# A new order list for a fused attention and two feed-forward stages, and products of 384 and 512 tokens

## The chip, the cores and the metric

The kernel runs on one core of a Trainium2 chip. TensorE (PE) multiplies matrices, VectorE (DVE) and ScalarE (ACT) work on elements and can read PE's results from PSUM, GpSimd (POOL) works on elements in SBUF alone, and SyncE (SP) issues nearly all DMAs. Each engine works through its own list of instructions in order and waits on semaphores for the others. The metric is the time of one execution in microseconds (us); the kernel before took 354.3 us, the median of three runs (353.45 to 354.36).

## The reference, cut to what matters

Two sequences of 448 tokens, 12 heads of 64, model width 768, inner width 1024. Causal attention, then a feed-forward stage that mixes each token with the one before it, then a feed-forward stage with a convolution of width 3 along the tokens:

```
attn = softmax(causal(q @ k.T / 8)) @ v            # per head
x    = attn, heads side by side                    # (2, 448, 768)
xk   = mu_k * x + (1 - mu_k) * x_prev              # x_prev: the token before
xr   = mu_r * x + (1 - mu_r) * x_prev
x2   = sigmoid(xr @ w_r) * (relu(xk @ w_k)**2 @ w_v)
h    = relu(x2 @ w_in)
out  = (h * sigmoid(conv3(h))) @ w_out
```

All five weight matrices arrive as 64-bit floats and are turned into 32-bit ones on the chip.

## The kernel before, in words

Attention is cut into 12 jobs: two sequences times six pairs of heads. A job's steps carry the names that stand in the order list. `Lk` and `Lv` load q, k and v (SP). `kqT` transposes q and k on PE, `kC.k` and `kC.q` copy the result out of PSUM. `sc.2` and `sc.1` are the scores on PE in 64x64 tiles, in two parts. `red` (DVE) adds the mask and finds the row's extreme, `exp` (ACT) exponentiates and sums, `rec` (DVE) inverts the sums, `norm` scales the probabilities, mostly on POOL. `T.a` and `T.b` transpose the probabilities on PE, `C.aX` and the like copy them out, `V.a` and `V.b` multiply by v. From the result `mP` (a scaling) and `mD` (a scaled addition) make the mixed inputs: kind 1 for xr, kind 0 for xk.

For the feed-forward products every number is split into a high and a low part. `mH` and `mL` make those of xr, `k0:H` to `k11:L` those of xk (the numbers 0 to 5 are the six chunks of 128 features of the first sequence, 6 to 11 of the second). A chunk of a result then takes three products on PE: high by high, high by low, low by high. A weight slice `w0` to `w5` (of w_r) and `w6` to `w8` (the first three of w_k) has steps too: `L` loads it, `a` (ACT) to `e` build the 32-bit floats, `h` and `l` split them. `pr3.1.4` stands for w_r's slice 3, token part 1, chunk 4: three products. `sr3.1` copies the finished bank out of PSUM. `E0` to `E3` are the first two slices of w_k, 18 products each, for two token parts. `W` steps are products with nobody to read them, which keep PE running. A letter behind a slash names the engine: a for ACT, v for DVE, p for POOL.

What sets the order is the list ORDER: `issue` takes its tokens one by one, and PE, ACT, DVE and POOL keep that order under a manual schedule (lines 624 to 627). The loads in it are kept in order on SP as well. Buffers are handed out from short lists as steps ask for them: eight PSUM banks, three buffers for raw q and k, four for v, two for raw weights, two for converted ones, four for split ones. Behind ORDER the rest of w_k, w_v and the second stage follow: for w_k and w_v the scheduler places the instructions, for the last stage a second list, LATE.

The other w_k and all w_v products are cut into a part of 512 tokens and one of 384 (lines 672 to 680). The w_r products and E0 to E3 are cut by sequence, 448 and 448:

```
TOK = [slice(b * S, (b + 1) * S) for b in range(B)]
```

Of the kernel before, what the change touches and what calls it, by code (L numbers as in the profile page):

```python
# [19 lines left out]
def kernel(  # L20
# [457 lines left out]
    class Slice:  # L478
# [22 lines left out]
        0:Lk W0 sm:L W*2 0:kqT 0:kC.k/a sm:a 1:Lk 0:kC.q/v W*2 0:sc.2 W*1 1:kqT sm:n 0:red.0 0:red.5 0:red.2 0:red.3  # L501
        0:exp.0 0:sc.1 1:kC.k/v 2:Lk 0:exp.5 1:kC.q/a 0:exp.2 1:sc.2 0:red.6 0:exp.3 0:red.1 0:red.4 0:exp.1 0:exp.4
        2:kqT 1:red.5 1:red.2 2:kC.k/v 1:red.0 0:exp.6 1:red.3 3:Lk 1:sc.1 2:kC.q/a 0:Lv 0:rec sm:T 2:sc.2 1:exp.2
        1:exp.5 0:norm.2/p 1:red.1 1:red.4 3:kqT 1:exp.1 1:exp.0 0:norm.4/p 1:exp.3 sm:C 0:norm.1/p 1:red.6 3:kC.q/v
# [4 lines left out]
        0:V.b 1:T.b 4:kC.q/a 3:exp.6 2:norm.5/p 2:norm.1/p 4:sc.1 3:red.1 2:norm.3/p 3:exp.5 0:V.a 3:red.3 1:C.bY/v
        2:norm.6/p w1:a 2:norm.0/p 2:norm.2/p w1:b/p 3:red.2 3:red.4 1:C.bX/v 1:C.aX/v 4:red.4 3:exp.3 2:norm.4/p  # L510
        0:mP.1/a 5:Lk 3:exp.4 4:red.1 2:T.a 3:exp.2 4:sc.2 2:T.b 3:exp.1 0:mP.0/v 2:C.aX/a 4:red.6 2:C.aY/a 3:rec
        w1:c 3:norm.3/p 3:norm.0/p 5:kqT 4:exp.1 4:red.3 4:red.0 2:C.bX/v 4:exp.4 5:kC.k/v 0:mD.1 3:norm.5/p
# [551 lines left out]
```

## Time and profile before

| | us |
|---|---|
| median of three runs | 354.3 (353.45 to 354.36) |
| profiled execution, from its first to its last instruction (its time as a run isn't recorded) | 351.6 |
| PE busy | 345.2 (98%) |
| DVE busy | 306.9 (87%) |
| ACT busy | 235.1 (67%) |
| POOL busy | 90.3 (26%) |
| last value product of attention ends | 90.03 |
| first product of w_k starts | 120.5 |

The profile is of one execution. Its span runs from the first to the last instruction; the rest of a run's time lies around it. Matmuls overlap, so a stretch in which PE is busy throughout can still hold short waits; those are seen in the chain of work that ended last, which is followed back from the end: its pieces are counted from the start of one instruction to that of the next, so that a piece divided by its count gives the pace of a product.

### The profile page before, as it was taken

What the parts mean: (1) busy time and instruction counts of PE and PEld (TensorE: products, weight loads), DVE (VectorE), ACT (ScalarE), POOL (GpSimd) and SP (SyncE); (2) the same over time, 40 slices, a digit from 0 to 9 for tenths busy, and PEclk for the clock granted to TensorE, in tenths of its full rate; (3) what the DMA queues carried; (4) which work ended last, traced back from release to release, by engine and by line L of the source; (5) the groups of instructions that cost most, each with busy time, mean ns of one, the idle gap of its engine ahead of it and who ended that gap; (6) DMA issues with size and microseconds to landing.
All of it is one profiled execution on the core that took longest, in us unless ns stands there. A gap on an engine that the chain in (4) does not pass through costs nothing.

```text
span 351.6 us, 7196 instructions
## 1 busy us (share of the span) xinstructions
PE 345.2 (98%) x2682; PEld 309.2 (88%) x2682; DVE 306.9 (87%) x629; ACT 235.1 (67%) x515; POOL 90.3 (26%) x149
## 2 busy tenths in 40 slices
PE   7999999999999999999999999999999999999996
PEld 7678788888999998998889999988988999999995
DVE  2999999999889878989999998997998999897741
ACT  2999999999533276767786464354756877766501
POOL 3386986667435000000000000000000000368100
PEclk9999999999999999999999999999999999999999
DMA  5686597442033155347455434543232200379623
GB/s 132 146 222 144 127 222 213 90 116 93 7 95 106 66 180 181 121 148 240 142 187 171 156 101 173 179 143 128 89 103 79 89 2 0 67 134 202 138 91 135
DMA packets 63228, 45.33 MB, mean 129 GB/s; under 512 B 34752, under 2 KB 62156, under 8 KB 63192
## 3 DMA queue, kind: packets, MB, share of 16 engines
q1 hardware_dynamic: 59352, 40.68, 38.7%
q0 software_dynamic: 2912, 3.96, 6.6%
q8 instruction: 21, 0.34, 0.4%
q10 hardware_dynamic: 928, 0.23, 0.3%
q14 instruction: 15, 0.12, 0.1%
HBM read 38.17 MB, written 2.75 MB: 116 GB/s over the span
## 4 chain that ended last, share of the span: by engine, by line
PE 95%; DVE 1%; DMA 1%; POOL 1%; SPq 1%; issue 1%; ACT 0%; POOLq 0%
PE pk L66 17%; PE pv L66 17%; PE pr L66 13%; PE A L66 7%; PE po L391 6%; PE s L321 4%; PE B L66 4%; PE c L66 2%; PE Yb L363 2%; PE D L66 2%; PE Xa L363 2%; PE W L561 1%; PE q L300 1%; PE ph5l L66 1%; PE ph6l L66 1%; PE ph4l L66 1%
## 5 line engine op out<-in xcount | busy, mean ns | idle before, releaser
L887 POOL DMA_DIRECT2D s<-g x12 | 12.7, 1177 | 194.9 <-ACT st L87 188.6
L343 ACT ACTIVATE p<-e,st 128x448 f32<-128x448 f32 (+6 forms) x84 | 42.1, 507 | 1.7 <-DVE st L334 1.5
L72 POOL TENSOR_SCALAR p<-p,st 128x64 f32<-128x64 f32 (+6 forms) x70 | 34.6, 512 | 20.7 <-DVE st L334 11.4
L334 DVE CUSTOM_DVE_ANT_0 e<-s,mask 128x192 f32<-128x192 f32 (+6 forms) x84 | 31.6, 415 | 0.4 <-ACT p L343 0.2
L391 PE MATMUL po<-pt,v 128*64 128x128 f32 (+4 forms) x384 | 24.0, 277 | 0.0
L807 DVE SCALAR_TENSOR_TENSOR cv<-hT,cw,cv 128x448 f32<-128x448 f32 x32 | 21.5, 681 | 2.7 <-ACT cv L804 2.6
L391 PEld LDWEIGHTS po<-pt,v 128*64 128x64 f32 x384 | 20.0, 137 | 3.3 <-issue 0.3
L321 PE MATMUL s<-kT,qT 64*64 64x384 f32 (+6 forms) x336 | 22.1, 386 | 0.5 <-DVE kT L79 0.2
L321 PEld LDWEIGHTS s<-kT,qT 64*64 64x64 f32 x336 | 14.9, 132 | 6.6 <-ACT qT L79 0.7
L343 ACT ACTIVATION_READ_ACCUMULATOR p<-e,st 128x1 f32 x84 | 16.3, 194 | 0.0
L91 POOL TENSOR_TENSOR xr<-m,xr 128x448 fp32r<-128x448 f32 x10 | 12.0, 1198 | 2.1 <-ACT xr L87 1.7
L87 ACT ACTIVATE x<-xv 128x512 fp32r<-128x512 f32 (+1 forms) x12 | 6.8, 573 | 8.1 <-DVE xv L706 8.0
L811 ACT ACTIVATE cv<-cv 128x448 f32<-128x448 f32 x16 | 9.1, 571 | 3.2 <-DVE cv L807 3.2
L999 ACT ACTIVATE o<-A 128x384 f32<-128x384 f32 x3 | 1.5, 491 | 14.7 <-PE A L66 14.6
L804 ACT ACTIVATE cv<-hT,cw 128x448 f32<-128x448 f32 x16 | 10.7, 668 | 0.5 <-DVE g L91 0.3
L813 DVE TENSOR_TENSOR cv<-cv,hT 128x448 f32<-128x448 f32 x16 | 9.9, 621 | 1.2 <-ACT cv L811 1.2
L91 DVE TENSOR_TENSOR k<-a,k 128x512 fp32r<-128x512 f32 (+2 forms) x16 | 9.9, 619 | 0.0
L66 PE MATMUL pv<-k,wv0hl 128*128 128x512 f32 (+1 forms) x48 | 9.9, 364 | 0.0
L66 PE MATMUL pv<-k,wv4hl 128*128 128x512 f32 (+1 forms) x48 | 9.8, 363 | 0.0
L66 PE MATMUL pv<-k,wv2hl 128*128 128x512 f32 (+1 forms) x48 | 9.8, 363 | 0.0
L66 PE MATMUL pv<-k,wv3hl 128*128 128x512 f32 (+1 forms) x48 | 9.8, 363 | 0.0
L66 PE MATMUL pv<-k,wv5hl 128*128 128x512 f32 (+1 forms) x48 | 9.8, 363 | 0.0
(516 smaller groups left out, 1105.0 us busy)
## 6 DMA issues: line engine op xcount, KB each, us to landing
rqk<-in_q_dram SPq DMA_DIRECT2D x24, 112.0 KB, 2.8
rqk<-in_k_dram SPq DMA_DIRECT2D x22, 112.0 KB, 3.0
v<-in_v_dram SPq DMA_DIRECT2D x24, 96.0 KB, 3.0
s<-g POOLq DMA_DIRECT2D x12, 192.0 KB, 3.8
wo6raw<-g POOLq DMA_DIRECT2D x8, 192.0 KB, 4.8
wv0raw<-in_moe_w_v_dram SPq DMA_DIRECT2D x1, 1024.0 KB, 4.8
wv1raw<-in_moe_w_v_dram SPq DMA_DIRECT2D x1, 1024.0 KB, 4.9
wv2raw<-in_moe_w_v_dram SPq DMA_DIRECT2D x1, 1024.0 KB, 5.0
```

Source lines behind the costliest of these rows:

```text
L66: nc.tensor.matmul(ps_out, x, y, start=first and i == 0, stop=last and i == 2, skip_group_check=more,)
L72: nc.gpsimd.tensor_scalar(out_, in_, s, 1.0, ALU.mult, ALU.mult)
L91: e.tensor_tensor(out_, x, f32(h), ALU.subtract)
L321: nc.tensor.matmul(held[self.name(f"s{f}")][1][h, o:z], qT[r, i * LO:(i + 1) * LO], kT[r, :(i + 1) * LO], start=True, stop=True,)
L334: nc.vector.tensor_tensor_reduce(t[:, :w], used(self.name(f"s{f}"))[:, o:z], mask[:, S - w:], -SCALE, 3e38, ALU.add, ALU.min, self.st[:, 0 ...
L343: nc.scalar.activation(p[:, :w], self.s[i][:, :w], AF.Exp, bias=self.st[:, 0, i:i + 1], scale=-1.0, accum_out=self.st[:, 1, i:i + 1],)
L363: nc.tensor.transpose(o[:, u * LO:(u + 1) * LO], self.p[i][r, k0:k0 + P], ident[r, r])
L391: nc.tensor.matmul(self.T["po"][j * D:(j + 1) * D, 1 + i * LO - z:1 + (i + n) * LO], self.v[:, kc, j], self.T["pt"][:, a - z:a + n * LO], ...
L804: nc.scalar.activation(a, x[:, 0:S], AF.Copy, scale=cw[:, f:f + 1])
L807: nc.vector.scalar_tensor_tensor(a, x[:, j:S + j], cw[:, j * NF + f:j * NF + f + 1], a, ALU.mult, ALU.add)
L813: (nc.gpsimd if eng == "p" else nc.vector).tensor_tensor(a, a, hc, ALU.mult)
L887: nc.gpsimd.dma_start(out=dst, in_=f32(x), accum_op=ALU.add)
```

## The change

The list ORDER is replaced by another one with the same 712 steps. Only their order, the engine behind the slash and the places of the loads differ. Two lines of each:

```
-        0:Lk W0 sm:L W*2 0:kqT 0:kC.k/a sm:a 1:Lk 0:kC.q/v W*2 0:sc.2 W*1 1:kqT sm:n 0:red.0 0:red.5 0:red.2 0:red.3
-        sr3.0/v w8:d pr5.0.5 w8:e E1 w7:e w7:h w7:l/v E2 sr0.1/a w8:h sr5.0/v w8:l/v E3
+        W0 W*2 0:Lk sm:L 0:kqT 0:kC.k/v 1:Lk sm:a sm:n 2:Lk 3:Lk 0:kC.q/a W*1 W*2 0:sc.2 0:red.3 0:exp.3 0:red.2
+        pr5.0.5 w6:l/p E0 k8:H/p k8:L/p k6:L/p k7:L/p k10:H/a sr5.1/a k11:L/p k10:L/p E3 E1 sr5.0/a E2 w8:l/p
```

And the w_r products and E0 to E3 take token parts of 384 and 512, across the border of the sequences:

```
+    PART = [slice(0, 3 * P), slice(3 * P, NT)]
+
+    def width(t):
+        return t.stop - t.start
...
     def xr_products(e, b, c):
         if c == 0:
             bank(f"pr{e}_{b}", 1)
-        products(held[f"pr{e}_{b}"][1][:, :S], [slices[e].t], xr, TOK[b], NC, c)
+        t = PART[b]
+        products(held[f"pr{e}_{b}"][1][:, :width(t)], [slices[e].t], xr, t, NC, c)
...
-        copy(eng, sr[e][:, TOK[b]], used(f"pr{e}_{b}")[:, :S])
+        t = PART[b]
+        copy(eng, sr[e][:, t], used(f"pr{e}_{b}")[:, :width(t)])
...
-            pk_banks[f, b] = bank(f"pk{f}_{b}", 1)[:, :S]
+            t = PART[b]
+            pk_banks[f, b] = bank(f"pk{f}_{b}", 1)[:, :width(t)]
             for c in range(NC):
-                products(pk_banks[f, b], [slices[NE + f].t], [xk[i] for i in range(NC)], TOK[b], NC, c)
+                products(pk_banks[f, b], [slices[NE + f].t], [xk[i] for i in range(NC)], t, NC, c)
...
-        pks = [(TOK[b], pk_banks[f, b]) for b in range(B)] if f < 2 else token_mm(f"pk{f}", w, xk, False)
+        pks = [(PART[b], pk_banks[f, b]) for b in range(B)] if f < 2 else token_mm(f"pk{f}", w, xk, False)
```

How the steps by engine change over the whole list: `mP` on ACT 12 to 18 and on DVE 12 to 6; `norm` on POOL 70 to 72, on ACT 7 to 11, on DVE 7 to 1; low parts of xk (`k:L`) on POOL 3 to 11 and on DVE 9 to 1; low parts of weight slices on POOL 3 to 6 and on DVE 6 to 3; `sr` copies on ACT 7 to 10 and on DVE 5 to 2.

SP's queue at the start. `rqk_4` is the raw q and k of job 4, `wr1raw` the first slice of w_r, `v_0` the first buffer for v. Before:

```order
L286 DMA rqk_3_299<-in_q_dram 64x7x64 x2
L286 DMA rqk_3_299<-in_k_dram 64x7x64 x2
L292 DMA v_0_112<-in_v_dram 128x3x64 x2
L293 DMA v_0_112<-in_v_dram 64x2x64
L286 DMA rqk_4_393<-in_q_dram 64x7x64 x2
L286 DMA rqk_4_393<-in_k_dram 64x7x64 x2
L159 DMA wr1raw_517<-in_moe_w_r_dram 128x6x128
```

The same place in SP's queue of the changed kernel:

```order
L290 DMA rqk_3_199<-in_q_dram 64x7x64 x2
L290 DMA rqk_3_199<-in_k_dram 64x7x64 x2
L290 DMA rqk_4_248<-in_q_dram 64x7x64 x2
L290 DMA rqk_4_248<-in_k_dram 64x7x64 x2
L159 DMA wr1raw_347<-in_moe_w_r_dram 128x6x128
L296 DMA v_0_112<-in_v_dram 128x3x64 x2
L297 DMA v_0_112<-in_v_dram 64x2x64
```

Job 4's four loads and the weight slice have moved ahead of the first loads of v.

PE where the last w_r products meet the first w_k products (`pr5_0` is slice 5, part 0; `pk0_0` slice 0 of w_k, part 0; `x3` three products). Before:

```order
L66 MATMUL pr4_0_2088<-xr5_111,wr4hl_2053 128x448 x3
L66 MATMUL pr5_0_2145<-xr4_110,wr5hl_2093 128x448 x3
L66 MATMUL pk0_0_2216<-xk0_2039,wk0hl_2174 128x448 x3
L66 MATMUL pk0_0_2216<-xk1_2007,wk0hl_2174 128x448 x3
L66 MATMUL pk0_0_2216<-xk2_2047,wk0hl_2174 128x448 x3
```

And PE in the changed kernel, from the last w_r product into E0 and E3 (`pk2`, `pk3` are the slices behind the list, `pk1_1` is E3):

```order
L66 MATMUL pr5_0_2096<-xr5_111,wr5hl_2055 128x384 x3
L66 MATMUL pk2_0_2364<-xk0_2109,wk2hl_2148 128x512
L66 MATMUL pk2_1_2365<-xk0_2109,wk2hl_2148 128x384
L66 MATMUL pk0_0_2229<-xk0_2109,wk0hl_2197 128x384 x3
...
L66 MATMUL pk0_0_2229<-xk5_2117,wk0hl_2197 128x384 x3
L66 MATMUL pk1_1_2257<-xk0_2109,wk1hl_2092 128x512 x3
L66 MATMUL pk1_1_2257<-xk1_2061,wk1hl_2092 128x512
L66 MATMUL pk2_0_2364<-xk0_2109,wk2hl_2148 128x512
L66 MATMUL pk2_1_2365<-xk0_2109,wk2hl_2148 128x384
L66 MATMUL pk1_1_2257<-xk1_2061,wk1hl_2092 128x512 x2
```

The widths are 384 and 512, E3 follows E0, and the scheduler has set eight products of the slices 2 and 3 between them.

POOL at the end of the list (`xr` and `xk` L83 are high parts, L91 low parts, `wk0hl` the split of w_k's slice 0). Before, from the last input of w_r on:

```order
L91 TENSOR_TENSOR xr3_109<-m_9_1922,xr3_109 128x448
L83 TENSOR_SCALAR xk0_2039<-mixed0_100 128x448 x2
L83 TENSOR_SCALAR xk5_2060<-mixed5_105 128x448
L83 TENSOR_SCALAR xk3_2111<-mixed3_103 128x448
L91 TENSOR_TENSOR xk1_2007<-mixed1_101,xk1_2007 128x448
L140 TENSOR_SCALAR wk0c_2109<-wk0c_2109 128x768
L83 TENSOR_SCALAR xk3_2111<-mixed3_103 128x448
L91 TENSOR_TENSOR xk2_2047<-mixed2_102,xk2_2047 128x448
L91 TENSOR_TENSOR xk5_2060<-mixed5_105,xk5_2060 128x448
```

And POOL in the changed kernel, the same stretch but for its last two rows:

```order
L91 TENSOR_TENSOR xr3_109<-m_9_1977,xr3_109 128x448
L91 TENSOR_TENSOR xk1_2061<-mixed1_101,xk1_2061 128x448
L91 TENSOR_TENSOR xk3_2089<-mixed3_103,xk3_2089 128x448
L91 TENSOR_TENSOR xk0_2109<-mixed0_100,xk0_2109 128x448
L91 TENSOR_TENSOR xk5_2117<-mixed5_105,xk5_2117 128x448
L91 TENSOR_TENSOR xk2_2191<-mixed2_102,xk2_2191 128x448
L91 TENSOR_TENSOR xk4_2077<-mixed4_104,xk4_2077 128x448
L91 TENSOR_TENSOR wk0hl_2197<-wk0c_2127,wk0hl_2197 128x768
L83 TENSOR_SCALAR xk2_2191<-mixed2_102 128x448
L91 TENSOR_TENSOR xk2_2191<-mixed2_102,xk2_2191 128x448
L91 TENSOR_TENSOR xk0_2109<-mixed0_100,xk0_2109 128x448
L91 TENSOR_TENSOR xk1_2061<-mixed1_101,xk1_2061 128x448
```

The low parts of xk now stand on POOL in one row, with the low part of w_k's slice 0 among them; behind the rows shown come those of chunks 5 and 4 and of slice 2.

## Rows read from the trace of the kernel before

**Rows 1.** The page: busy us of each engine, share of the span, instructions.
```profile
PE 345.2 (98%) x2682; PEld 309.2 (88%) x2682; DVE 306.9 (87%) x629; ACT 235.1 (67%) x515; POOL 90.3 (26%) x149
```
**Rows 2.** Table of stretches: us, then each engine's busy us (instructions), clock, DMA.
```profile
5.30:25.00 19.70, 18.64 (x311) 14.21 (x312) 18.39 (x80) 17.34 (x60) 9.05 (x20) 1.00 0.77 185
...
44.00:90.00 46.00, 46.00 (x698) 39.15 (x694) 44.20 (x135) 44.13 (x126) 33.25 (x50) 1.00 0.53 140
90.00:120.60 30.60, 30.60 (x152) 27.80 (x149) 27.99 (x39) 12.76 (x21) 11.29 (x11) 1.00 0.24 78
```
**Rows 3.** Chain that ended last, after attention: start us, us, what.
```profile
90.10 30.57 PE pr L66 x147
120.66 3.72 PE pk L66 x18
...
125.00 54.77 PE pk L66 x270
179.77 58.03 PE pv L66 x288
237.79 4.12 PE ph0l L66 x18
...
242.60 3.14 PE ph0h L66 x18
```
**Rows 4.** The same chain, the start.
```profile
1.74 3.66 PE W L561 x18
...
10.81 3.31 DMA rqk<-in_k_dram
14.87 0.64 PE W L561 x4
...
22.35 2.31 POOL p L72 x5
```
**Rows 5.** The same chain, w_r inside attention, first and last of six pieces.
```profile
46.34 1.41 PE pr L66 x6
...
79.00 3.23 PE pr L66 x15
```
**Rows 6.** The page's groups: line, engine, operation, tiles, count | busy us, mean ns.
```profile
L343 ACT ACTIVATE p<-e,st 128x448 f32<-128x448 f32 (+6 forms) x84 | 42.1, 507 | 1.7 <-DVE st L334 1.5
L72 POOL TENSOR_SCALAR p<-p,st 128x64 f32<-128x64 f32 (+6 forms) x70 | 34.6, 512 | 20.7 <-DVE st L334 11.4
L334 DVE CUSTOM_DVE_ANT_0 e<-s,mask 128x192 f32<-128x192 f32 (+6 forms) x84 | 31.6, 415 | 0.4 <-ACT p L343 0.2
```
**Rows 7.** PE in order of time, 25.3 to 26.5: start us, us, instruction.
```profile
25.34 0.99 PE L321 MATMUL s<-kT,qT 64*64 64x384 f32 x16
26.26 0.27 PE L363 MATMUL Yb<-ident,p 64*128 64x64 f32 x1
```
**Rows 8.** DVE's groups by shape, a scaling.
```profile
L74 DVE TENSOR_SCALAR mixed<-po,mu 128x448 f32<-128x448 f32 x7 | 4.7, 677 | 0.0
```
**Rows 9.** POOL's groups by shape, the subtractions.
```profile
L91 POOL TENSOR_TENSOR xr<-m,xr 128x448 fp32r<-128x448 f32 x10 | 12.0, 1198 | 2.1 <-ACT xr L87 1.7
...
L91 POOL TENSOR_TENSOR xk<-mixed,xk 128x448 fp32r<-128x448 f32 x3 | 4.8, 1608 | 2.8 <-ACT xk L87 2.8
...
L91 POOL TENSOR_TENSOR wr0hl<-wr0c,wr0hl 128x768 fp32r<-128x768 f32 x1 | 1.8, 1828 | 2.0 <-ACT wr0hl L87 2.0
```
**Rows 10.** ACT's groups by shape, a copy and a split.
```profile
L79 ACT COPY sr<-pr 128x448 f32<-128x448 f32 x7 | 3.7, 525 | 1.7 <-PE pr L66 1.6
...
L87 ACT ACTIVATE wk0hl<-wk0c 128x768 fp32r<-128x768 f32 x1 | 0.8, 847 | 2.8 <-DVE wk0c L146 2.8
```
**Rows 11.** POOL in order of time, 104 to 112.
```profile
107.27 3.27 POOL L91 TENSOR_TENSOR xk<-mixed,xk 128x448 fp32r<-128x448 f32 x2
```
**Rows 12.** DVE in order of time, 107 to 112.
```profile
107.75 1.78 DVE L144 SCALAR_TENSOR_TENSOR wk0c<-wk0raw,wk0c 128x768 int32<-128x768 int32 x1
...
110.95 0.95 DVE L146 SCALAR_TENSOR_TENSOR wk0c<-wk0raw,wk0c 128x768 int32<-128x768 int32 x1
```

More of the change, by code (lines that the diff above doesn't have):

```diff
@@ L551 @@
[L551 to L553 removed]
+        W0 W*2 0:Lk sm:L 0:kqT 0:kC.k/v 1:Lk sm:a sm:n 2:Lk 3:Lk 0:kC.q/a W*1 W*2 0:sc.2 0:red.3 0:exp.3 0:red.2
+        0:sc.1 1:kqT 4:Lk 0:exp.2 sm:T 0:red.0 0:exp.0 1:kC.k/a 0:red.5 0:red.6 0:exp.6 1:kC.q/v 1:sc.2 0:red.1
@@ new lines @@
+        0:red.4 0:exp.1 sm:C 0:exp.4 1:red.3 1:red.0 1:red.2 1:red.5 0:exp.5 0:rec 2:kqT 1:sc.1 2:kC.k/a 1:exp.2
+        1:exp.3 W*2 0:norm.5/p 2:kC.q/v 0:norm.1/p 1:red.6 Wend 2:sc.2 1:red.1 w1:L 1:red.4 1:exp.0 2:red.5
+        1:exp.5 0:norm.6/p 0:norm.0/p 0:norm.4/p 0:norm.3/p 1:exp.1 2:red.3 0:Lv 3:kqT 3:kC.k/v 3:kC.q/v
+        0:norm.2/p 2:red.0 0:T.a 1:exp.4 1:exp.6 1:rec 1:norm.3/p 5:Lk 2:sc.1 2:red.4 2:exp.5 1:norm.2/p 0:T.b
+        2:red.1 1:Lv 0:C.aX/a 2:exp.0 0:C.bY/v 0:C.aY/a 2:exp.4 2:red.6 0:C.bX/v 2:exp.1 1:norm.6/p 4:kqT
@@ new lines @@
+        4:norm.4/p 2:mP.0/v 3:V.a 6:kC.q/a 5:exp.1 1:mL/p 5:red.4 7:kC.q/v 1:mP.0/a 3:V.b 1:mD.0 3:mP.1/a
+        4:norm.2/p 2:mD.0 4:T.a 4:C.aX/a 6:sc.2 6:red.0 6:red.5 2:mH/p 4:Lv 4:norm.3/p 5:Lv 2:mL/p 6:sc.1
+        5:exp.0 w2:L 5:exp.4 5:exp.2 4:T.b 4:C.aY/v 3:mP.0/a 5:rec 6:red.6 5:norm.3/p 7:sc.1 6:exp.5 4:C.bX/a
+        5:norm.2/p 6:exp.6 4:V.a 6:red.4 5:norm.1/p 6:exp.4 5:norm.6/p w1:h 4:C.bY/v 8:kqT 9:Lk 6:red.3 10:Lk
+        4:V.b 3:mD.0 6:red.1 5:norm.5/p 6:exp.3 3:mD.1 8:kC.k/a 6:red.2 7:red.1 5:norm.4/p 5:T.b 6:exp.0
@@ new lines @@
+        w2:b/p 6:C.bY/v 7:norm.2/a 5:mD.1 9:kC.q/a pr1.0.4 6:C.bX/a 7:norm.1/p 8:red.3 7:norm.0/p 10:kqT
+        7:norm.3/a 9:kC.k/v w2:c 8:exp.6 8:red.2 7:T.b 5:mP.0/a w2:d 8:exp.1 7:norm.6/p 8:exp.2 6:V.a 8:red.5
+        7:C.bX/a 7:C.bY/a 6:V.b 8:red.0 w2:e 7:norm.5/p 8:exp.0 5:mH/p 9:sc.1 10:kC.q/a w2:h w2:l/p 5:mD.0
+        10:kC.k/v 9:sc.2 8:exp.5 8:exp.4 5:mL/p 9:red.1 9:exp.1 9:red.6 10:sc.1 9:red.4 9:red.3 7:T.a 9:red.2
+        8:exp.3 8:rec w0:a 7:C.aY/v 9:exp.2 pr2.0.0 pr2.0.1 9:exp.4 pr2.0.2 w0:b/p 9:red.5 pr2.0.3 9:exp.5
@@ new lines @@
+        10:exp.1 11:red.4 6:mP.0/v 8:V.b 10:exp.3 9:norm.2/p 8:V.a 10:exp.5 pr0.0.0 9:norm.4/p 10:rec w3:h
+        9:norm.6/p 9:norm.5/a pr0.0.1 pr0.0.2 11:red.6 w3:l/p pr0.0.3 pr0.0.4 pr0.0.5 8:mP.1/a 11:red.3 6:mD.0
+        9:T.b 11:red.2 10:norm.6/p 10:norm.5/a sr0.0/v 7:mD.1 9:C.bX/v 9:norm.0/a w4:a 9:T.a 9:C.bY/a
+        10:norm.2/p 11:exp.1 w5:L pr3.0.0 pr3.0.1 pr3.0.2 11:exp.6 11:exp.3 10:norm.3/p 11:exp.2 pr3.0.3 pr3.0.4
+        9:C.aX/v 11:red.5 11:exp.4 7:mH/p 10:norm.4/p pr3.0.5 10:norm.1/p 11:exp.5 9:C.aY/v 11:red.0 11:exp.0
```

83 lines of the change are left out of this document (32 added, 51 removed).

## The prediction

> **What bounds the kernel now.** I read the page's busy shares first [rows 1]: PE is busy 345.2 of 351.6 us, DVE 87%, ACT 67%. A busy PE alone proves nothing, because overlapping matmuls count as busy; the table of stretches [rows 2] and the chain that ended last settle it. From 44 to 90 us (attention) PE is busy the whole time, and so nearly are DVE (44.20 of 46) and ACT (44.13): three engines in balance. From 90 to 120.6 us (w_r products) only PE is full. In the chain [rows 3] the last attention product is followed without a gap by 147 w_r products in 30.57 us, then by the w_k products to 179.8 us and the w_v products: from 90 us to the last stage the path is PE's own work, and the end moves by what PE's list becomes shorter or waits less. Before about 25 us the path leaves PE [rows 4]: it waits for the fourth job's DMA (10.81 to 14.12 us), passes time in keep-warm products (0.64 us at 14.87), and at 22.35 us stands behind five normalisations on POOL. So there are three places: the price of a w_r or w_k product, the start, and the hand-over from attention to w_k.
>
> The granted clock is 1.00 in every stretch [rows 2], the level of 2.4 GHz, and the new list keeps the keep-warm products (14 tokens' worth in both), so I count nothing for the clock.
>
> **Form of the products.** 216 w_r products and 72 products of the first two w_k slices go from 448 tokens each to half at 384 and half at 512. Same columns in total. A 448 product costs 3.72 us / 18 = 206.7 ns in the chain. The other 216 w_k products already alternate 512 and 384: 270 took 54.77 us, less 54 x 0.2067 leaves 43.61, or 201.9 each; w_v's 288 took 58.03, 201.5 each [rows 3]. One width alone: 4.12 / 18 = 228.9 ns at 512, 3.14 / 18 = 174.4 at 384, mean 201.7. Gain 5.0 ns x 288 = **1.44 us**, all on the path. Both widths stand in the trace, so a loss is excluded; bounds 1.1 (the w_r stage's own 30.57 / 147 = 208.0 is 1.3 ns above 206.7, and the new widths may carry that too) to 1.9 (208.0 against 201.5).
> The Trainium skill speaks against this gain: "TensorE: Matmul & The Clock Gate", section "Back-to-back issue gap", gives an isolated warm product N/2.4 + 2.5 ns, linear in N with one constant per product. By that, 448 + 448 and 384 + 512 cost the same and this term would be zero; the trace disagrees, 206.7 against 201.7 ns.
>
> **Pieces of w_r inside attention.** Each time PE goes from small tiles to 128x128 products and back it loses something: six pieces there (the first and the last in [rows 5]) take 14.60 us for 66 products, 0.96 more than 66 x 0.2067, or 0.16 per piece. The new list has 72 products in four pieces (15, 21, 18, 18). Gain 2 x 0.16 = **0.32 us**.
>
> **The start, 5.3 to 25 us.** On SP the fifth job's q/k loads move ahead of the first w_r slice and the first v loads; jobs 1 to 3 keep their places, so their DMAs land as now. On ACT and DVE the copies of k and q swap engines (each 0.5 to 0.6 us), the small table's first step goes ahead of a copy (at most 0.3 us, less if it runs while PE still transposes), and three of the five later keep-warm tokens move directly behind the first transposes, where six records at 0.20 us (3.66 / 18 [rows 4]) hold PE to about 7.2 us instead of 6.8. I walked the lists by hand with durations of this trace: a job costs DVE 31.6 / 12 = 2.6 us of reductions, ACT 42.1 / 12 = 3.5 us of exponentials, POOL seven normalisations at 0.51 us [rows 6]. The first normalisation comes at 13.2 us (13.55 now), the first transposed probabilities at 15.3 (15.45). The fourth job's transposes come at 14.7 us, after its DMA landed at 14.12, so that wait is gone; the fifth job's come at 17.5, the list having loaded it 2.7 us earlier. What is late next is POOL's normalising of jobs 1 and 2, at 19.8 and 24.5 us. When PE begins job 2's first transposed block the clock stands at 25.5 us, against 26.26 now with the same work done [rows 7]. Gain **0.75 us**. Bounds: 2.0 (the ten later keep-warm records at 0.20, which fill time that PE waits) to a loss of 0.9 (one part of the scores, 25.34 to 26.26 [rows 7], falling behind).
>
> **The rest of attention.** PE runs there end to end [rows 2], so little waiting is left to go, and new waits can come. To the last value product the list takes four scalings of 0.68 us [rows 8], six normalisations and a weight step off DVE, and adds two copies, two splits and one more weight step to it: about 2.5 us less; ACT's sum stays within 0.2 us; POOL's is near equal. DVE was the fullest, so I take **0.3 us** gain; bounds 2.4 gain (DVE's whole relief) to 2.0 loss (ACT or POOL late where DVE no longer is).
>
> **The hand-over, where POOL gets work.** Call the end of the last value product V (90.03 us now). Behind it stand 108 products of 512 and 36 of 384, 31.0 us, then the first two w_k slices. Eleven of the twelve low-part subtractions of w_k's inputs stand on POOL (three now), one on DVE (nine now). On ACT the copy of w_r slice 0 waits for PE until V + 19.8; queued behind it are high parts of w_k inputs, and POOL's subtractions wait for those. So POOL starts its row of five at V + 21.6; at 1.15 to 1.20 us each (w_r inputs: mean 1.198 [rows 9]) it ends at V + 27.4, just when ACT has the high part of w_k slice 0 (two copies of 0.53 us and the split of 0.84 [rows 10] after the wait for slice 4 at V + 25.6). Its low part costs 1.83 [rows 9]: V + 29.3, before PE arrives at V + 31.0. Then a short step of about 0.6 and five more: V + 35.6 to 35.9; PE wants the last but one at V + 31.0 + 3.1 + 4 x 0.69 = V + 36.9. About 1 us to spare. The scheduler also put eight products of slices 2 and 3 in between; they are moved, not added. Right behind V, the w_r inputs of the last three jobs are due 2 to 3.5 us later and are ready within some tenths of that. I take a loss of **0.2 us**; bounds 0 to 3.2, from the dearer mean of such subtractions, below.
>
> **Sum.** 1.44 + 0.32 + 0.75 + 0.30 - 0.20 = 2.6 us less than the profiled execution's 351.6, so a span of 349.0. The runs' median is 354.3; what lies around the span, 2.7 us, doesn't change. Forecast 351.7 us. Later stages keep their lists; DVE reaches them with less behind it, so I count nothing there.
>
> **Rivals.**
> - *POOL too slow at the hand-over (slower).* The three subtractions of w_k inputs on POOL in this trace took a mean of 1.608 us [rows 9], not 1.2; the two at 107.27 (3.27 us together) [rows 11] lie beside a DVE step of 1.78 us; one like it 3 us later takes 0.95 [rows 12]. With L each, the last is ready at V + 24.0 + 10 L and PE wants it at V + 36.9: a wait of 10 L - 12.9. At 1.608 that is 3.2 us, the result 351.7 + 3.2 = 354.9; the gain is used up at 1.55, and from 1.66 it is slower beyond doubt. Against it: DVE is out of list work from about V + 19.5, and only four conversion steps of slice 3 come beside POOL's row (V + 30.6 to 33.9).
>  The Trainium skill, "SBUF — State Buffer", section "Who interferes with whom", says that a DVE instruction with two SBUF inputs and a GpSimd one that reads SBUF block each other; the rows at 107 us agree. By that rule only DVE's last two conversion steps could hold POOL, about 2 x 0.95 us, of which 1 us is spare: 352.6.
> - *ACT sets the pace of attention.* It is as full as DVE [rows 2] and loses no work. Then the start's gain, the rest's and the product form inside attention are given back as waits, and what remains is the form behind V, 222 x 5.0 = 1.1 us: 353.2, on the border of no change. For it: 44.13 of 46. Against: PE, too, is full there, and its list is what shrinks.
> - *The product form changes nothing.* If a product costs one constant and a price per column, 228.9 and 174.4 [rows 3] make 0.426 ns a column and 10.9 ns, a 448 product costs 201.7 too, and the 206.7 has another cause that stays: 351.7 + 1.4 = 353.1. Against it: both w_k slices of 448 stand directly before the mixed ones and cost 206.7.
> - *DVE was the real brake of attention.* Its 2.5 us come off the path instead of 0.3: 349.5.
>
> **Chances.** Forecast 0.60 (its own range 350.2 to 353.0), POOL 0.11, ACT 0.10, form 0.06, DVE the brake 0.13. About 0.3% (1.06 us) is what a measurement of this kernel can tell from no change, so faster means below 353.2, slower above 355.4. Faster: 0.59 + 0.13 + 0.03 = 0.75; same: 0.01 + 0.09 + 0.03 + 0.04 = 0.17; slower: 0.07 of POOL and 0.01 of ACT, 0.08. The range 349.3 to 354.2 leaves out about half of the POOL and a third of the DVE case, and the ends of the forecast.
>
> **What would show it.** The w_r pieces at 174 and 229 ns a product in place of 207; four w_r pieces inside attention; job 2's first transposed block near 25.5 us and the last value product near 87.8; the first w_k product 31 us behind it, with no wait named POOL before PE's w_k products. Wrong would be: PE waiting in the first two w_k slices, a subtraction on POOL near 1.6 us there, or ACT without gaps to 88 us while PE waits.

## The result, and the profile after

The changed kernel takes 357.3 us (median of 4 runs, 356.4 to 357.6), the kernel before 354.3 beside it: a ratio of 1.0081 (95% interval 1.0063 to 1.0099). By that ratio it is slower by 2.9 us where 2.6 us of gain were forecast; the time lies above the range.

The page shows first that the three full engines have little more to do: PE is busy as long as before, DVE 7.6 us less, ACT 7.4 us more. POOL is busy 13.1 us more [rows 1].

```profile
PE 345.5 (97%) x2682; PEld 308.1 (87%) x2682; DVE 299.3 (84%) x607; ACT 242.5 (68%) x529; POOL 103.4 (29%) x157
```

The table of stretches, cut at the changed kernel's own borders (last value product at 94.65 us, first w_k product at 125.71), answers [rows 2]. Columns: stretch, length, busy us of PE, PEld, DVE, ACT, POOL, clock, DMA.

```profile
44.00:94.60 50.60, 47.84 (x730) 40.85 (x726) 49.10 (x138) 46.52 (x133) 37.94 (x57) 1.00 0.48 132
94.60:125.70 31.10, 31.10 (x150) 26.67 (x145) 18.89 (x27) 20.34 (x35) 12.27 (x11) 1.00 0.41 127
125.70:141.80 16.10, 16.10 (x81) 14.46 (x81) 13.88 (x15) 8.21 (x14) 9.29 (x6) 1.00 0.19 57
```

Before, PE was busy 46.00 of 46 us of the middle stretch; now it is idle for 2.8 us, and the engine that is full is DVE, 49.10 of 50.6. Behind it PE is full again. The chain that ended last says the same (start us, us, what) and answers [rows 3]:

```profile
91.05 3.67 PE po L395 x64
94.72 31.15 PE pr L66 x144
125.87 58.12 PE pk L66 x288
183.99 58.03 PE pv L66 x288
```

Behind the last value product everything is as forecast: 31.06 us to the first w_k product (31.0 forecast), 58.12 us of w_k in place of 58.49, no wait on POOL. From w_k's fifth slice on, the two traces are equal (201.07 and 201.06 us to the end). The whole loss, 4.6 us, lies ahead of the last value product: 94.65 where 87.8 was forecast and 90.03 stood before.

These are two single executions. In nearly all runs the time is 1.7 to 1.9 us above the span, so the execution profiled before took some 353.4 us, 0.9 below the median of its kernel; the changed kernel's took 357.62, 0.3 above. Of the 4.2 us between the two spans (351.6 and 355.8) some 1.2 go with the choice of executions, and the 2.9 of the medians are what the change costs. (The 2.7 us that the forecast put around the span are thus 1.8, and 0.9 for a quick execution; the forecast time, taken from the median, stands.)

One row explains why DVE is full there. The sum of exponentials of each job gets 1e-9 added on DVE, a 128x7 instruction. In the groups of the kernel before (columns as in [rows 6]):

```profile
L350 DVE TENSOR_SCALAR st<-st 128x7 f32<-128x7 f32 x12 | 2.0, 165 | 0.2 <-ACT p L343 0.2
```

and of the changed one:

```profile
L354 DVE TENSOR_SCALAR st<-st 128x7 f32<-128x7 f32 x12 | 5.3, 442 | 0.0
```

The same twelve instructions take 3.3 us more. Five of them last 0.35 to 1.50 us, each until an instruction of POOL ends; such an instruction is called held below. The longest, in order of time on DVE, and what POOL does meanwhile:

```profile
74.05 0.42 DVE L338 CUSTOM_DVE_ANT_0 e<-s,mask 128x256 f32<-128x256 f32 x1
...
74.39 1.50 DVE L354 TENSOR_SCALAR st<-st 128x7 f32<-128x7 f32 x1
75.92 0.20 DVE L355 RECIPROCAL st<-st 128x7 f32<-128x7 f32 x1
```

```profile
74.04 1.82 POOL L91 TENSOR_TENSOR wr0hl<-wr0c,wr0hl 128x768 fp32r<-128x768 f32 x1 [4.26 <-ACT wr0hl L87]
```

POOL's subtraction ends at 75.86, the add at 75.89. The others end 24 to 28 ns behind a POOL instruction in the same way. The chain that ended last runs through all five (3.9 us together); its three longest pieces there:

```profile
54.80 0.72 DVE st L354
64.13 1.01 DVE st L354
74.47 1.43 DVE st L354
```

The reduction at 74.05, which reads s from PSUM, runs under the same subtraction at its usual length. In the kernel before no add began under a POOL instruction with more than 0.02 us left; two RECIPROCALs did, with 1.00 and 0.26 us left, and were not held (0.20 us each). The first, and POOL beside it:

```profile
39.09 0.20 DVE L351 RECIPROCAL st<-st 128x7 f32<-128x7 f32 x1
```

```profile
38.95 1.15 POOL L91 TENSOR_TENSOR xr<-m,xr 128x448 fp32r<-128x448 f32 x1
```

That gave the first theory (A): the new list puts POOL's low-part subtractions where DVE's small adds come, DVE waits for POOL, and everything behind the add on DVE's list waits too. The Trainium skill, "SBUF — State Buffer", section "Who interferes with whom", names tensor_scalar among the DVE instructions that can take the ports shared with GpSimd, and says that the one that starts later is blocked until the other ends; the rows above agree.

### The profile page after: what moved, and what is told of

Read it like the earlier page. It is cut to its first block, busy times and chain, and to the rows that moved or that the text cites. A ratio compares the mean times of both kernels' runs of the same rounds, so it can differ in the third digit from the quotient of the medians.

```text
span 355.8 us, 7177 instructions
## 1 busy us (share of the span) xinstructions
PE 345.5 (97%) x2682; PEld 308.1 (87%) x2682; DVE 299.3 (84%) x607; ACT 242.5 (68%) x529; POOL 103.4 (29%) x157
## 4 chain that ended last, share of the span: by engine, by line
PE 78%; DVE 13%; ACT 6%; issue 1%; POOL 0%; POOLq 0%; ACTq 0%; DVEq 0%
PE pk L66 16%; PE pv L66 16%; PE pr L66 10%; PE A L66 7%; DVE e L338 4%; ACT p L347 4%; PE B L66 4%; PE c L66 2%; DVE pt L79 2%; PE D L66 2%; PE W L567 2%; DVE m L420 1%; DVE st L354 1%; PE ph5l L66 1%; PE ph6l L66 1%; PE ph4l L66 1%
## 5 line engine op out<-in xcount | busy, mean ns | idle before, releaser
L347 ACT ACTIVATE p<-e,st 128x384 f32<-128x384 f32 (+6 forms) x84 | 42.2, 508 | 3.9 <-DVE st L338 3.7
L72 POOL TENSOR_SCALAR p<-p,st 128x320 f32<-128x320 f32 (+6 forms) x72 | 35.8, 516 | 20.8 <-DVE st L355 18.1
L338 DVE CUSTOM_DVE_ANT_0 e<-s,mask 128x256 f32<-128x256 f32 (+6 forms) x84 | 31.9, 413 | 1.1 <-PE s L325 0.9
L325 PE MATMUL s<-kT,qT 64*64 64x128 f32 (+6 forms) x336 | 22.2, 385 | 1.8 <-DVE qT L79 1.7
L91 POOL TENSOR_TENSOR xk<-mixed,xk 128x448 fp32r<-128x448 f32 x11 | 15.0, 1401 | 18.5 <-ACT xk L87 18.4
L91 DVE TENSOR_TENSOR k<-a,k 128x384 fp32r<-128x384 f32 (+1 forms) x16 | 10.8, 682 | 1.4 <-ACT k L87 1.4
L896 POOL DMA_DIRECT2D wo6raw<-g x8 | 9.1, 1189 | 3.9 <-ACT wo6raw L921 3.9
L91 POOL TENSOR_TENSOR xr<-m,xr 128x448 fp32r<-128x448 f32 x8 | 9.6, 1199 | 1.5 <-ACT xr L87 1.4
L367 PE MATMUL Yb<-ident,p 64*128 64x64 f32 x96 | 8.5, 227 | 1.4 <-DVE st L338 0.8
```

Source lines behind the costliest of these rows:

```text
L72: nc.gpsimd.tensor_scalar(out_, in_, s, 1.0, ALU.mult, ALU.mult)
L91: e.tensor_tensor(out_, x, f32(h), ALU.subtract)
L325: nc.tensor.matmul(held[self.name(f"s{f}")][1][h, o:z], qT[r, i * LO:(i + 1) * LO], kT[r, :(i + 1) * LO], start=True, stop=True,)
L338: nc.vector.tensor_tensor_reduce(t[:, :w], used(self.name(f"s{f}"))[:, o:z], mask[:, S - w:], -SCALE, 3e38, ALU.add, ALU.min, self.st[:, 0 ...
L347: nc.scalar.activation(p[:, :w], self.s[i][:, :w], AF.Exp, bias=self.st[:, 0, i:i + 1], scale=-1.0, accum_out=self.st[:, 1, i:i + 1],)
L896: nc.gpsimd.dma_start(out=dst, in_=f32(x), accum_op=ALU.add)
```

## Experiments

Times are medians; the ratio is to the kernel before on the same chip.

| run | us | ratio (95%) | last value product ends | held on DVE before it |
|---|---|---|---|---|
| before | 354.3 | 1 | 90.03 | 0.89 us |
| changed | 357.3 | 1.0081 (1.0063-1.0099) | 94.65 | 4.26 |
| e1 add made a RECIPROCAL | 354.8 | 1.0013 (1.0001-1.0025) | 92.15 | 0.65 |
| e2 add left out | 354.9 | 1.0018 (1.0010-1.0027) | 92.11 | 0.73 |
| e3 before, add left out | 354.5 | 1.0005 (0.9994-1.0016) | 90.80 | 0.35 |
| e4 before, form alone | 354.6 | 1.0008 (0.9999-1.0016) | 91.25 | 0.91 |
| e5 two POOL steps moved | 356.9 | 1.0080 (1.0068-1.0092) | 93.73 | 3.69 |
| e6 e1 with 448 | 361.8 | 1.0223 (1.0205-1.0242) | 93.80 | not summed |
| e7 e1, job 11's reciprocals earlier | 355.6 | 1.0046 (1.0034-1.0058) | 92.05 | 1.58 |
| e8 e1, job 7's load earlier | 354.9 | 1.0025 (1.0009-1.0040) | 91.90 | 0.66 |
| e9 before, mixed form | 353.3 | 0.9975 (0.9964-0.9986) | 90.34 | 0.88 |
| e10 e7, no add, two steps later | 355.5 | 1.0037 (1.0022-1.0051) | 90.32 | 1.48 |
| e11 e10, w_r order | 355.5 | 1.0039 (1.0025-1.0054) | 90.43 | 1.47 |
| e12 e11, slice 5 earlier | 357.7 | 1.0098 (1.0072-1.0123) | 89.92 | not summed |

"Held" sums, up to the last value product, what DVE instructions take beyond the lower quartile of their own form, where that is over 90 ns, whatever the cause. The ends and the holds are of one profiled execution each. Diffs of the order list are cut to the tokens around a moved step.

**e1 and e2: the add.**

```diff
-            nc.vector.tensor_scalar(self.st[:, 2], self.st[:, 1], 1e-9, None, ALU.add)
-            nc.vector.reciprocal(self.st[:, 2], self.st[:, 2])
+            nc.vector.reciprocal(self.st[:, 2], self.st[:, 1])
+            nc.vector.reciprocal(self.st[:, 2], self.st[:, 1])
```

e2 has the second of the two new lines only. The 1e-9 is left out in both.

> The changed kernel with one instruction swapped in each of the twelve jobs: the 128x7 add of 1e-9 to the sums of exponentials, on DVE (SBUF in, SBUF out), becomes a second RECIPROCAL of the same seven columns. DVE keeps as many instructions (0.20 us in place of 0.165 each), the lists don't change. In the changed kernel's trace five of the twelve adds last 0.35 to 1.50 us, each until a POOL instruction that began before it ends, 3.33 us more than twelve adds took before; two RECIPROCALs that began under a POOL instruction in the kernel before took 0.20 us. Theory A (these holds are the loss; DVE sets the pace, 49.1 of 50.6 us busy from 44 us to the last value product): 2.3 to 3.3 us of it come back, last value product near 91.8, time 354.6 (354.0 to 355.2). Rival B (the list waits on ACT and on its own order, the holds lie beside that): 357.3 within 0.5. Rival C (the 384-token products took work of PE out of attention, where DVE and ACT set the pace, and put it behind): also no change, or at most 1 us.

> The changed kernel without the add: one RECIPROCAL straight from the sums (each is at least 1, so the 1e-9 is below its last bit). DVE loses twelve instructions. Theory A: as e1 and up to 2.4 us of DVE's work less, 353.6 (352.6 to 354.6). Rivals B and C: 12 x 0.165 = 2 us of DVE's work less of which little is on the path, 356.8 (356.3 to 357.3).

e1 measured 354.8, as theory A said (354.6). DVE issues as many instructions, and each of the 24 takes 0.19 to 0.20 us, though twelve of them began under a POOL instruction that had 0.10 to 1.42 us left. The one under the subtraction that held the longest add:

```profile
72.97 0.19 DVE L354 RECIPROCAL st<-st 128x7 f32<-128x7 f32 x1
```

```profile
72.53 1.86 POOL L91 TENSOR_TENSOR wr0hl<-wr0c,wr0hl 128x768 fp32r<-128x768 f32 x1 [3.70 <-ACT wr0hl L87]
```

The stretch up to the last value product is 2.45 us shorter, with PE's idle time there down from 2.8 to 1.25:

```profile
44.00:92.15 48.15, 46.90 (x731) 40.68 (x726) 46.07 (x138) 46.38 (x133) 38.75 (x57) 1.00 0.50 137
```

So 2.4 (by the ratios) to 2.5 us of the 2.9 us of loss were the held adds; rivals B and C fall as reasons for that part. The chain changes with them: from 26 to 92 us its longer pieces are 41 us of DVE, 15 of ACT and 7 of PE in the changed kernel, and 35 us of PE, 19 of ACT and 5 of DVE in e1.

e2 misses (354.9, not 353.6): the 2.4 us of DVE's work that go beside the hold bring nothing that shows. Its trace shows two reasons. From w_k's fifth slice to the end it takes 201.46 us where e1 takes 201.10, and the difference lies behind the last instruction of ACT; the five kernels without the add (e2, e3, e10, e11, e12) all take 201.46 to 201.56 there, the others but e6 201.00 to 201.10. Why is not known; it hides some 0.4 us of what these five gain. And PE came 1.2 us earlier out of the start than in e1, and then waited for job 7's keys:

```profile
36.89 0.25 PE L304 MATMUL k<-ident,rqk 64*128 64x64 f32 x1 [1.30 <-DMA rqk<-in_k_dram]
```

**e3: the kernel before without the add** (the same edit as e2).

> The kernel before without the add. There none of the twelve adds was held (0.155 to 0.172 us each), so only DVE's 2.0 us of work go, while PE is busy from end to end from 25 us on. Theory A: little, 353.8 (353.3 to 354.3), far less than e2 gains on the changed kernel. If it is DVE's amount of work and not the holds that counts, the kernel before gains as much as the changed one, 2.5 us or more: 351.8 or less.

354.5, no change, or some 0.5 us of gain without the longer end (201.54 us, 201.06 before): little beside what e1 gains, so it is the hold that costs, not the add.

**e4: the form alone,** the changed kernel's code (384 and 512) with the list of before. The diff is cut; the copies of w_r's banks and E0 to E3 take PART too.

```diff
+    PART = [slice(0, 3 * P), slice(3 * P, NT)]
-        products(held[f"pr{e}_{b}"][1][:, :S], [slices[e].t], xr, TOK[b], NC, c)
+        t = PART[b]
+        products(held[f"pr{e}_{b}"][1][:, :width(t)], [slices[e].t], xr, t, NC, c)
```

> The kernel before with the product form alone: the parts of 384 and 512 tokens for w_r and the first two w_k slices, on the list of before. The forecast's term (5.0 ns a product, 288 products, all on the path): 354.3 - 1.4 = 352.9. Rival C: the 66 w_r products inside attention have 384 tokens and lose 2.2 us of PE's time there, where DVE and ACT are as full as PE, so the last value product stays near 90.0; behind it stand 42 products of 384 and 108 of 512, 32.0 us in place of 31.2, and the two w_k slices give back 0.36: 354.8 (354.3 to 355.3).

354.6, a ratio of 1.0008 (0.9999 to 1.0016): the forecast's 1.4 us are not there, rival C's number (354.8) is. Where no wait of PE was listed between 40 and 95 us before, three are now (engine, line, waited for: us in total, times, longest):

```profile
PE Yb L367 <- DVE mixed L420: 0.5, 1, 0.5
PE q L304 <- ACT pt L79: 0.4, 1, 0.4
PE Yb L367 <- DVE pt L79: 0.2, 1, 0.2
```

From the first w_r piece to the last value product it takes 44.13 us, with 1.8 us less in those pieces; before it took 43.76. The shorter products leave PE waiting for DVE and ACT. Behind, more is left to do, as the chain shows: 31.77 us in place of 30.57 [rows 3], against 0.4 less in w_k.

```profile
91.32 31.77 PE pr L66 x147
123.09 3.12 PE pk L66 x18
126.21 0.52 PE pr L66 x3
126.73 54.95 PE pk L66 x270
```

**e5: POOL's two subtractions moved** behind a normalisation, everything else of the changed kernel kept.

```diff
-        w2:l/p 5:mD.0 10:kC.k/v 9:sc.2 8:exp.5 8:exp.4 5:mL/p 9:red.1
+        w2:l/p 5:mD.0 10:kC.k/v 9:sc.2 8:exp.5 8:exp.4 9:red.1
-        8:norm.3/p pr2.0.4
+        8:norm.3/p 5:mL/p pr2.0.4
-        w0:l/p 7:Lv
+        7:Lv
-        9:norm.1/p 10:exp.1
+        9:norm.1/p w0:l/p 10:exp.1
```

> The changed kernel, every instruction kept, the add too: on POOL's list the two instructions under which the two longest adds were held (the low part of job 5's w_r input, 1.16 us, and of w_r slice 0, 1.83 us) move behind the first one or two normalisations that wait for that add, so that POOL is idle when the add comes. Theory A (the hold by POOL is the loss): the adds of jobs 8 and 9 fall from 1.00 and 1.50 us to 0.165; of the 2.2 us on DVE 0.8 to 2.2 come back, part of it lost because PE's products of slice 0 now wait for that slice's later low part: 355.8 (355.1 to 356.5). Rival B (holds beside the path): 357.3 or slower.

356.9, a miss; beside the kernel before its ratio, 1.0080, is that of the changed kernel. The two adds fell to 0.17 and 0.16 us, but the moved subtraction now holds another DVE instruction (0.95 us else), and job 10's add is held for 0.52:

```profile
75.40 2.33 DVE L146 SCALAR_TENSOR_TENSOR wr3c<-wr3raw,wr3c 128x768 int32<-128x768 int32 x1
```

```profile
75.09 1.83 POOL L91 TENSOR_TENSOR wr0hl<-wr0c,wr0hl 128x768 fp32r<-128x768 f32 x1
```

The sum of holds went only from 4.26 to 3.69 us, and PE waited 0.6 us for slice 0. The run did not separate A from B as planned; it shows that moving POOL's work moves the hold.

**e6: e1 with 448 tokens.** `PART = TOK` in place of the two slices.

> e1 with the product form of before: all w_r products and those of the first two w_k slices at 448 tokens, on the changed kernel's list. The forecast's term (5.0 ns a product, all on the path): 354.8 + 1.4 = 356.2. Rival C (products inside attention fill time that PE has over, products behind it are on the path): the 72 products inside attention grow by 72 x 32.7 ns = 2.35 us into some 3 us of waits, the 144 behind it shrink from 31.0 to 29.8 us, the w_k slices cost 0.36 more: 354.8 - 0.85 = 354.0 (353.5 to 354.9).

361.8 misses both. 4.5 us of it lie in the last stage (176.5 us from the first w_v product to the end, 172.0 in e1): there the scheduler laid out DVE's, ACT's and SP's work in another order, and PE waited 2.3 us for a w_in slice and 0.9 for an input. That part says nothing on the form. Up to w_k's fifth slice e6 is 1.9 us behind e1. Its 72 w_r products inside attention take 2.1 us more and the stretch from the first of them to the last value product 1.0 us more (38.98 and 37.96 us); so in this list about half of the products' length inside attention was on the path, where rival C expected nothing. Behind it the 144 products are 1.2 us shorter, as C had it, but PE takes 1.1 us more than these products cost (it waits for w_r inputs and a slice), and w_k took 0.4 more. Together e6 is 1.3 us dearer there than e1, near the forecast's 1.4 and far from C's gain; the other 0.6 of the 1.9 lay ahead of the first piece. Nearly all of PE's idle time in attention is gone:

```profile
44.00:93.80 49.80, 49.39 (x740) 41.97 (x737) 47.00 (x140) 47.37 (x134) 38.99 (x58) 1.00 0.50 134
```

**e7 and e8: two waits of e1.**

```diff
-        6:mH/p 8:mD.1 11:rec 11:norm.1/p
+        6:mH/p 11:rec 8:mD.1 11:norm.1/p
```

> e1 with one DVE step moved: in the last job the reciprocals stand ahead of the scaling of job 8 (they stood behind it, and it waited 1.33 us in e1 for an ACT step that comes after all seven exponentials of job 11). Theory D (beside the holds, the changed list itself makes PE wait at the end of attention, 0.38 and 0.73 us at 86.4 and 87.4 us, because DVE waits for ACT in list order): the four normalisations on ACT start some 1 us earlier, last value product 0.5 to 1.1 us earlier, 354.0 (353.6 to 354.4). If something else is late there (the copies on ACT behind those normalisations): 354.8.

355.6, slower than e1. The wait at 86.4 us went (16 transposes in 0.52 us, 1.47 in e1), and the next one took its place: a conversion step of w_r slice 4 on DVE now began under a POOL subtraction and was held, and the copy behind it came late, so that the last 64 value products took 4.88 us (3.67).

```profile
87.00 1.50 DVE L142 TENSOR_SCALAR wr4c<-wr4c 128x768 int32<-128x768 int32 x1
88.53 0.96 DVE L144 SCALAR_TENSOR_TENSOR wr4c<-wr4raw,wr4c 128x768 int32<-128x768 int32 x1
89.41 0.68 DVE L79 COPY pt<-Yb 128x512 f32<-128x512 f32 x1
```

```profile
86.83 1.14 POOL L91 TENSOR_TENSOR xr<-m,xr 128x448 fp32r<-128x448 f32 x1 [1.15 <-ACT xr L87]
```

e8 moved `7:Lk` ahead of `3:Lv` on SP.

> e1 with one load moved: the q/k of job 7 stand ahead of job 3's v loads on SP. In e2 PE came 1.2 us earlier out of the start and then waited 1.30 us for job 7's keys (36.9 us); in e1 and the changed kernel, whose PE came later, there was no such wait. Theory E (the start's gain is given back to the load queue): where the profile has the early start, PE reaches job 8's transposes at 43.3 us instead of 44.5, and the median falls by 0 to 0.8: 354.4. If PE then only waits for DVE and ACT later: 354.8, the same.

354.9, the same. In its profile PE came late out of the start again, so the wait for job 7's keys couldn't show; theory E is left untested there.

**e9: the form only where it is on the path.** The list of before, with

```diff
+    RPART = [TOK] * 4 + [PART] * 2
-        t = PART[b]
+        t = RPART[e][b]
```

in both w_r functions; E0 to E3 take PART.

> The list of before, with the new product form only where every product stands behind the last value product: w_r slices 4 and 5 and the first two w_k slices at 384 and 512 tokens, w_r slices 0 to 3 (whose first half runs inside attention) at 448. If 5.0 ns a product is right on the path (forecast and rival C alike): 144 x 5.0 ns = 0.7 us, last value product as before, 354.1 - 0.7 = 353.4 (352.9 to 353.8), faster than both kernels. If the form brings nothing even there: 354.1.

353.3, a ratio of 0.9975 (0.9964 to 0.9986): faster than both kernels. Attention is as before, and PE is full in it; the chain behind has 30.34 and 58.07 us where [rows 3] has 30.57 and 58.49.

```profile
90.41 30.34 PE pr L66 x147
120.75 3.12 PE pk L66 x18
...
124.39 54.95 PE pk L66 x270
```

**e10 to e12: what else is late in the changed list.** e10 is e7 with e2's single RECIPROCAL and two steps of w_r slice 4 later; e11 and e12 each keep the edits of the one before.

```diff
-        11:T.a w4:c 11:C.aY/a 10:V.a w4:d 11:C.bY/v
+        11:T.a 11:C.aY/a 10:V.a 11:C.bY/v w4:c w4:d
```

> e7 without the add, and with two DVE steps of w_r slice 4 (the masking and the first merging step) moved behind the last copy of transposed probabilities of job 11 that stands on DVE. In e7 the first of them was held by a POOL subtraction (1.50 us in place of 0.55) and both stood ahead of that copy, so that the last value products took 4.88 us, not 3.67. Theory A: the hold goes, the copy comes some 2 us earlier, last value product near 90.9: 354.4 (353.9 to 354.9). If another instruction is then held or late in its place: 355.6 again.

The last value product came at 90.32 (90.9 expected), and the time stayed (355.5): PE then waited for the w_r inputs of jobs 9 to 11. Up to w_k's fifth slice e10 is 0.4 us ahead of e7 (152.07 and 152.48 us), and its longer end takes that back.

```profile
90.32 2.59 PE L66 MATMUL pr<-xr,wr3hl 128*128 128x512 f32 x10
93.63 0.96 PE L66 MATMUL pr<-xr,wr3hl 128*128 128x512 f32 x3 [0.73 <-POOL xr L91]
94.86 1.46 PE L66 MATMUL pr<-xr,wr3hl 128*128 128x512 f32 x5 [0.26 <-DVE xr L91]
```

e11 moves `pr1.1.0 pr1.1.1 pr1.1.2` ahead of `pr3.1.3`.

> e10 with nine products moved on PE behind the last value product: slice 1's products with the inputs of jobs 6 to 8 go ahead of slice 3's products with those of jobs 9 to 11. In e10 the last value product came at 90.32 us, 1.7 us earlier than in e7, but PE's next 18 products, which want all six inputs of the second sequence, took 5.84 us in place of 4.12, because the low parts of jobs 9 to 11 were ready only at 93.6, 94.8 and 95.5 us. Theory F (the changed list asks for the last jobs' w_r inputs first, so what attention gives PE waits for): the 1.7 us are kept, 355.5 - 1.7 = 353.8 (353.3 to 354.4), below the kernel before by 0.5. If another input is then late (w_r slices 4 and 5, or w_k's): 355.5.

Those waits went, and the time stayed (355.5): PE now waits 0.97 us at 103.5 for the low part of w_r slice 5, which is itself held:

```profile
103.02 1.90 DVE L91 TENSOR_TENSOR wr5hl<-wr5c,wr5hl 128x768 fp32r<-128x768 f32 x1
```

```profile
102.25 1.86 POOL L91 TENSOR_TENSOR xk<-mixed,xk 128x448 fp32r<-128x448 f32 x1 [8.54 <-DMA wk2raw<-in_moe_w_k_dram]
```

e12 moves `w5:l/v` from behind `k4:H/a` to behind `w5:h`.

> e11 with one more DVE step moved: the low part of w_r slice 5 stands ahead of the four conversion steps of w_k slice 1 instead of behind them. In e11 the 1.7 us that PE kept behind the last value product were lost at 103.5 us, where three products of slice 5 took 2.17 us and the next six 1.46: that low part began on DVE at 103.0 us and was itself held by a POOL subtraction (1.90 us, 0.95 in the changed kernel). If that was the last late thing: 355.5 - 1.5 = 354.0 (353.6 to 354.6). If DVE's list has something else late (w_k's first inputs, slice 1's conversion): 355.5.

357.7, slower. The low part began at 100.71 us, but a conversion step of w_k slice 1 was now held under a POOL subtraction (1.40 us, 0.56 in e11), the scaled additions that empty the attention results began at 105.47 (104.85 in e11), and PE waited 2.62 us for them:

```profile
106.30 1.63 PE L66 MATMUL pr<-xr,wr4hl 128*128 128x512 f32 x6 [2.62 <-DVE mixed L419]
```

Behind that wait the granted clock fell for a stretch (last section). The two of e12's six runs with a mean granted clock of 1.00 took 356.4 and 356.7 us, the four at 0.995 took 357.6 to 359.1, so a good part of its loss goes with the clock.

Four times a wait was taken away, and each time PE met the next one within some 10 us: three times for DVE, in e10 mostly for POOL.

## Why the prediction was wrong

**The step that failed** is "The rest of attention": "To the last value product the list takes four scalings ..., six normalisations and a weight step off DVE ...: about 2.5 us less", of which 0.3 was taken as gain, with a bound of 2.0 us of loss "(ACT or POOL late where DVE no longer is)". Counted at usual lengths DVE's instructions up to there fall by some 1.4 us, not 2.5 (a second weight step and a scaled addition were left out of the count), but 3.3 us of holds by POOL came on top. DVE was busy 81.52 us from 5.3 us to the last value product before and 84.75 after; without the table's holds that is 80.6 and 80.5, no relief to speak of. POOL's sum, called "near equal", rose from 58.21 to 61.08, ACT's by 1.1, not 0.2. e1 takes the held adds away with the list unchanged and gets 2.5 us back. The prediction had rows for such a mechanism ([rows 11, 12]) and used it only for DVE's two-input conversion steps at the hand-over; it never asked under which POOL instruction a small DVE step would begin in the new order.

**The form.** The price was right: 31.15 us for 108 and 36 products behind the last value product (31.0 forecast), w_k 0.37 us shorter, 5.0 ns a product. "All on the path" held only in part. On the list of before, shorter products inside attention let PE wait, and nothing is gained (e4); those behind it pay, 0.7 us expected and 1.0 measured in e9 (354.28 to 353.25, interval 0.5 to 1.3). On the changed list the form is worth about 1.3 us up to w_k's fifth slice (e6 against e1, one execution each), 1.0 of it inside attention. The prediction itself called attention "three engines in balance" [rows 2] and yet put every product there on the path.

**Fewer pieces** were four as forecast and cost what was forecast (21 products 3.84 us, 18 products 3.33 us in e1), but lie inside attention too.

**The start.** The 0.75 us came for the most part from a misreading. "26.26 now with the same work done" [rows 7] is the second block of transposes of job 2 in the kernel before; its first had run from 24.70:

```profile
24.70 0.27 PE Xa L363
```

In the new list job 2's first block comes ahead of that other one, so at this point PE has done 16 transposes less (all else is equal), worth the 0.64 us from 24.70 to 25.34. With the same work done the kernel before stands at 25.62, and 25.5 would have been a gain of 0.1. Measured were 26.88 us in the changed kernel and 25.70 to 26.95 in the nine runs on its list or a variant; the list of before, counted alike, has 25.62, and 25.95 to 26.47 in e3, e4 and e9. So no gain is seen. The scatter goes with PE's first products: the first 14 of this kind took 2.65 us before and 3.19 after, from the same list.

```profile
2.75 2.65 PE L561 MATMUL W<-ident 128*128 128x128 f32 x14
```

```profile
2.75 3.19 PE L567 MATMUL W<-ident 128*128 128x128 f32 x14
```

PE's pace doubles at 4.67 us in the profile before, and on the changed list, with the same PE instructions, anywhere from 5.29 (e2) to 7.56 us (e1). Where the start came early (e2), a load took it back.

**The hand-over** to w_k held: no wait on POOL, though its eleven subtractions took 1.40 us on average (the page's group), between the 1.2 and the 1.6 that were argued over. The first five took 5.62 us together, about as forecast; the five behind w_k's slice took 7.67, or 1.53 each, near the rival's 1.608, and ended at V + 37.8 instead of 35.9. PE didn't wait even so: the last five products of E3 began only at V + 38.8, behind products of slices 2 and 3. The group:

```profile
L91 POOL TENSOR_TENSOR xk<-mixed,xk 128x448 fp32r<-128x448 f32 x11 | 15.0, 1401 | 18.5 <-ACT xk L87 18.4
```

**Rivals.** In the changed kernel ACT was not the pace (46.52 of 50.6 us against DVE's 49.10). Without the held adds it may be part of it: e1 has ACT at 46.38 of 48.15 us, DVE at 46.07, PE at 46.90. Its 222 products behind V are 216 in the new list (144 and 72); the 1.1 us stay. "DVE was the real brake" had the engine right and the sign wrong. And "only PE is full" from 90 to 120.6 us overlooked DVE with 27.99 of 30.6 us there [rows 2]; it is in that stretch that e10 to e12 meet late steps of DVE.

**What stays open.** Without the held adds the changed list is at 354.8, still 3.1 us above the forecast. The form is not the reason there (e6). The start's 0.75 and the rest's 0.3 did not come; the cause of the other 2 us stays open. e7 and e10 to e12 show late steps on DVE up to 105 us wait by wait, but none of them makes the kernel faster. e1's chain points elsewhere: it holds 5 us of DVE and 19 of ACT from 26 to 92 us, with these two as ACT's longest pieces:

```profile
80.09 3.46 ACT p L347 x14
85.23 1.60 ACT p L76 x4
```

So the forecast's rival "ACT sets the pace of attention" is not excluded for this part; no run took work off ACT. Over e1, e7, e10, e5 and the changed kernel the time rises with the sum of holds by about 0.7 us per us (354.8 at 0.65, 357.3 at 4.26), which fits but is not proof for each.

## What to carry to other kernels

When a list moves work to POOL, look for the DVE steps from SBUF to SBUF that will begin while POOL runs: even a 0.17 us one costs POOL's whole remaining time, and a form that isn't held (here RECIPROCAL; the reduction that reads PSUM wasn't held either) takes that loss away (2.5 us here). A faster instruction pays where its engine alone is full; in a stretch where three engines are within 4% of full it may only move the wait, so price the two kinds of stretch apart. Taking away the wait that a profile shows is a forecast only when the next late thing on the same engine's list has been looked up.

## What the runs showed of the hardware beside that

A RECIPROCAL of 128x7 from SBUF to SBUF is not held by POOL (0.20 us each in e1, under POOL or not), while a TENSOR_SCALAR of the same shape is (0.35 to 1.50 us).

In e12 PE was busy 1.38 us of the 4 us from 103 us on, and the granted clock then fell to a mean of 0.66 over the next 5 us, so part of these ran at the level of 1.2 GHz (three products of 512 from 107.77 to 109.01, 1.24 us, 0.68 elsewhere):

```profile
103.00:107.00 4.00, 1.38 (x7) 0.99 (x6) 3.93 (x6) 1.85 (x5) 0.15 (x1) 1.00 0.07 11
107.00:112.00 5.00, 5.00 (x17) 3.95 (x16) 4.89 (x8) 2.30 (x4) 0.00 (x0) 0.66 0.48 155
```

At the start the first products run at 213 ns each until 4.67 to 7.56 us and at 112 behind that, with the clock column at 1.00 throughout: there the column doesn't show the pace.
